# Attention with a gated mixer on one core: two of four probability tiles turned by TensorE instead of by a DMA transpose

## Chip, cores, metric

One core of a Trainium2 chip, with its five engines: TensorE (PE), VectorE (DVE), ScalarE (ACT), GpSimd (POOL) and SyncE (SP), which issues most of the transfers. The metric is the device time of one execution in microseconds (us); lower is better. Each engine has its own instruction queue and works through it in order.

## What is computed

```python
kv_pool = kv.reshape(B, H // r, r, W // r, r, C).mean(axis=(2, 4))   # r = 4
k = v = kv_pool.reshape(B, -1, C) @ w_sr                             # 768 keys
s = scale * (q @ k.transpose(0, 2, 1))
s = s - s.max(-1, keepdims=True)
a = np.exp(s)
a /= a.sum(-1, keepdims=True) + 1e-09
x = a @ v                                                            # attention
gate = sigmoid(sum(conv_w[k] * x_padded[:, k:k + S] for k in range(5)))
out = (gate * (x @ w_val)) @ w_out
```

There are 4 batches of 12288 queries with 128 channels; each batch has 768 keys. Everything is float32. Values and probabilities enter the second product as pairs of float16 numbers, a high and a low half, so that little is lost.

## The kernel before

**Groups, tiles and steps.** A group is 512 queries; there are 96 groups, 24 to a batch, numbered by `gi`. A group has four tiles (`j` = 0 to 3) of 128 queries. The main loop (line 442) has one step for each tile, 384 in all. The order of the work is written out by hand, in that loop, and each engine's queue has it in this order. In the step of tile `j` of group `gi` stand, as far as they concern the change:

- On TensorE: `g_val` (L361, in step 1, a 128x512 float32 product of x and w_val for group gi-4), the score of the *next* tile (`score`, L251: six matmuls into a `[128, 768]` float32 PSUM tile `s`, of which there are three), in step 2 `g_out` (L371, the product with w_out), and a part of the product of probabilities and values for group gi-2 (`av_part`, L303). That product is 18 matmuls of 512 columns, cut into 6, 3, 3 and 6 for steps 0 to 3; the last part stands at the head of step 3, the others at the end of their steps.
- On VectorE: `g_h` in step 2 (L366), the row maximum of this tile (`row_max`, L257), the low half of the *previous* tile's probabilities (`p_lo`, L288), in step 3 `g_x` (L322: scales av by 1/z into x), and in step 1 `norm` of the group before (L270 and L271: z plus 1e-9, reciprocal).
- On ScalarE: exp of this tile, in place in PSUM, which also sums its rows into a column of z (`expo`, L263), then the high half of this tile's probabilities times 2^15, as float16 into an SBUF tile `hl` (`p_hi`, L282). Besides these it has `tap` (L330, steps 0 and 2), tanh (L357, step 1), the evacuation of the output (L381, step 3) and the rounding of q (L239, step 3).
- On GpSimd: the rest of the convolution over x (L332, L341) and the low part of q (L243).
- On SP: q's loads, the stores, and the following transfers.

**The turn of the probabilities.** The scores have queries on partitions, and the product with the values needs keys on partitions. `hl` holds high and low halves of two tiles, `[128, 2, 2, 768]` float16, in three buffers. After the low half of tile 1 and of tile 3, SP issues a DMA transpose of both tiles into `pt` (L294). There are two transposes a group; the last two tiles of the run are turned by one transpose each, 193 in all. `p_lo` is also the last reader of the PSUM tile `s`, so the score three tiles later waits for it.

**1/z on all partitions.** `norm` leaves the reciprocals as `[128 queries, 4 tiles]`; a DMA writes them to DRAM (`rd`, L272, in step 1), and a second one reads them back as one row, broadcast to 128 partitions (`rb`, L277, in step 3). `g_x` reads `rb` a group later.

**PSUM.** Eight banks: three `s` tiles of two banks, one bank for `av`, and one for everything else (`misc`, tile `m`): `g_val`, `g_out` and, when a new batch comes up, the projection of its keys and values. A new user of `misc` waits for the last reader of the one before.

**New batches.** In each batch's second group and after it, small steps prepare the next batch: one in each step 3 (pooling, products), the splits into high and low parts follow in step 0, `low()` after `p_lo` on VectorE.

**After the loop** (line 509 on) the last five groups are finished in another hand-written order.

Of the kernel before, what the change touches and what calls it, by code (L numbers as in the profile page):

```python
# [16 lines left out]
P = 128  # L17
GQ = 512
NT = GQ // P


class Group:
# [2 lines left out]

@with_exitstack
def attn_moe_kernel(ctx, tc, qT, kvT, w_sr, w_moe, outT):
    """qT, outT: [B, C, N]; kvT: [B, R, C, keys * R]; w_moe: [C, C + C + taps], the columns of
    w_val, w_out and conv_w transposed, as float64 bits (int64) or float32."""
    nc = tc.nc  # L30
    B, C, N = qT.shape
    NK, RR = kvT.shape[3] // R, R * R
# [14 lines left out]
    kvp = ctx.enter_context(tc.tile_pool(name="kvp", bufs=4))  # L47
    keys = ctx.enter_context(tc.tile_pool(name="keys", bufs=2))
    io = ctx.enter_context(tc.tile_pool(name="io", bufs=2))
    hlp = ctx.enter_context(tc.tile_pool(name="hlp", bufs=3))  # L50
    ptp = ctx.enter_context(tc.tile_pool(name="ptp", bufs=4))
    work = ctx.enter_context(tc.tile_pool(name="work", bufs=2))
    xp = ctx.enter_context(tc.tile_pool(name="xp", bufs=3))
# [8 lines left out]

    ident = const.tile([P, P], F32, name="ident")
    make_identity(nc, ident)
    wsr = const.tile([C, C], F32, name="wsr")
    wm = const.tile([C, NW], F32, name="wm")
    wval, wout, cwt = wm[:, 0:C], wm[:, C:2 * C], wm[:, 2 * C:]

    def load_moe():
        """Loads the weights; the steps that make float32 of float64's bits, rounded to nearest."""  # L70
        if w_moe.dtype == F32:
            nc.sync.dma_start(out=wm, in_=w_moe)
            return []
        raw = kvp.tile([C, HALF * R], F32, name="rows0", bufs=1).bitcast(I32)[:, :2 * NW]
        rest = kvp.tile([C, HALF * R], F32, name="rows1", bufs=1)
        nc.sync.dma_start(out=raw, in_=w_moe.bitcast(I32))
        words = raw.rearrange("c (n w) -> c w n", w=2)
        lo, hi = words[:, 0], words[:, 1]
        sign, ex, a, t = (rest.bitcast(I32)[:, i * NW:(i + 1) * NW] for i in range(4))
        low = rest[:, 4 * NW:5 * NW]  # L80
        v = nc.vector

        def two(out, in_, s1, op0, s2, op1):
            return lambda: v.tensor_scalar(out=out, in0=in_, scalar1=s1, scalar2=s2,
                                           op0=op0, op1=op1)

        def one(out, in_, s1, op):
            return lambda: v.tensor_single_scalar(out=out, in_=in_, scalar=s1, op=op)

        def both(out, x, y, op):  # L90
            return lambda: v.tensor_tensor(out=out, in0=x, in1=y, op=op)

        return [
            two(ex, hi, 20, ALU.logical_shift_right, 0x7FF, ALU.bitwise_and),
            two(ex, ex, -896.0, ALU.add, 0.0, ALU.max),
            two(ex, ex, 255.0, ALU.min, float(1 << 23), ALU.mult),
            two(a, hi, 0xFFFFF, ALU.bitwise_and, 3, ALU.logical_shift_left),
            two(t, lo, 29, ALU.logical_shift_right, 7, ALU.bitwise_and),
            both(a, a, t, ALU.bitwise_or),
            one(a, a, 0x3F800000, ALU.bitwise_or),  # L100
            one(sign, hi, -2147483648, ALU.bitwise_and),
            both(a, a, sign, ALU.bitwise_or),
            one(t, lo, 0x1FFFFFFF, ALU.bitwise_and),
            two(low, t, 2.0 ** -52, ALU.mult, 0.0, ALU.add),
            both(low.bitcast(I32), low.bitcast(I32), sign, ALU.bitwise_or),
            both(low, low, a.bitcast(F32), ALU.add),
            both(wm, low, ex.bitcast(F32), ALU.mult),
        ]
# [53 lines left out]
        return high, low  # L162

    def column_scale(st):
        """Steps for the power of two that brings the largest value of each column to
        [2^14, 2^15), on a diagonal, and what takes it and P's 2^15 out again."""
        big = small.tile([C, 1], F32, name="big")
        pw = small.tile([C, 1], F32, name="pw")
        up = small.tile([C, 1], I32, name="up")
        st["down"] = keys.tile([C, 1], F32, name="down")  # L170
        st["diag"] = keys.tile([C, C], F32, name="diag", bufs=1)
        v = nc.vector
        return [
            lambda: v.tensor_reduce(out=big, in_=st["vt"], axis=AX.X, op=ALU.max,
                                    apply_absolute_value=True),
            lambda: v.tensor_single_scalar(out=pw.bitcast(I32), in_=big.bitcast(I32),
                                           scalar=0x7F800000, op=ALU.bitwise_and),
            lambda: v.tensor_scalar_max(out=pw, in0=pw, scalar1=2.0 ** -90),
            lambda: v.tensor_scalar(out=up, in0=pw.bitcast(I32), scalar1=-1.0,
                                    scalar2=float(268 << 23), op0=ALU.mult, op1=ALU.add),  # L180
            lambda: v.tensor_scalar_mul(out=st["diag"], in0=ident, scalar1=up.bitcast(F32)),
            lambda: v.tensor_scalar_mul(out=st["down"], in0=pw, scalar1=2.0 ** -29),
        ]
# [35 lines left out]
        return steps + value_steps(st)  # L219

    def load_pair(g, n, parts=1):
        """Loads q for groups g and n with one transfer, or as many as parts."""
        q = io.tile([C, 2, GQ], F32, name="q")
        g.q, n.q = q[:, 0], q[:, 1]

# [29 lines left out]
    def row_max(g, j):  # L255
        nm = small.tile([P, 1], F32, name="nm")
        nc.vector.tensor_reduce(out=nm, in_=g.s[j], axis=AX.X, op=ALU.max, negate=True)  # L257
        g.nm[j] = nm

    def expo(g, j):  # L260
        if j == 0:
            g.z = small.tile([P, NT], F32, name="z")
        nc.scalar.activation(out=g.s[j], in_=g.s[j], func=AF.Exp, bias=g.nm.pop(j),  # L263
                             accum_out=g.z[:, j:j + 1])

    def norm(g):
        ze = small.tile([P, NT], F32, name="ze")
        r = small.tile([P, NT], F32, name="r")
        g.rd = dram.tile([P, NT], F32, name="rd")
        nc.vector.tensor_scalar_add(out=ze, in0=g.z, scalar1=1e-9)  # L270
        nc.vector.reciprocal(out=r, in_=ze)  # L271
        nc.sync.dma_start(out=g.rd, in_=r)  # L272

    def norm_rows(g):
        g.rb = work.tile([C, GQ], F32, name="rb", bufs=3)
        row = g.rd.rearrange("(o p) j -> o (p j)", o=1)
        nc.sync.dma_start(out=g.rb, in_=row.broadcast_to([C, GQ]))  # L277

    def p_hi(g, j):
        if j % 2 == 0:  # L280
            g.hl = hlp.tile([P, 2, 2, NK], F16, name="hl")
        nc.scalar.activation(out=g.hl[:, j % 2, 0], in_=g.s[j], func=AF.Copy, scale=2.0 ** 15)  # L282
        g.h2[j] = g.hl

    def p_lo(g, j, width=2):
        """The low half of tile j; then the transpose of the last `width` tiles."""
        hl = g.h2.pop(j)
        nc.vector.scalar_tensor_tensor(out=hl[:, j % 2, 1], in0=g.s.pop(j), scalar=2.0 ** 15,  # L288
                                       in1=hl[:, j % 2, 0], op0=ALU.mult, op1=ALU.subtract)
        if j == 1:  # L290
            g.pt = ptp.tile([P, NT, 2 * NCH, P], F16, name="pt")
        if j % 2 or width == 1:
            j0, i0 = j + 1 - width, j % 2 + 1 - width
            nc.sync.dma_start_transpose(  # L294
                out=g.pt[:, j0:j + 1].rearrange("p j k q -> p (j k) q"),
                in_=hl[:, i0:i0 + width].rearrange("p j a k -> p (j a k)"))

    AV_ORDER = [(v, k, a) for k in range(NCH) for v, a in (("vh", 0), ("vl", 0), ("vh", 1))]

# [17 lines left out]
        g.tap = {}  # L317

    def g_x(g, av, c0=0, c1=GQ):
        tiles = lambda a: a.rearrange("c (j p) -> c j p", p=P)  # L320
        rows = g.rb.rearrange("c (p j) -> c j p", j=NT)[:, c0 // P:c1 // P]
        nc.vector.scalar_tensor_tensor(out=tiles(g.x[:, HALO + c0:HALO + c1]), in0=tiles(av),  # L322
                                       scalar=g.st["down"], in1=rows,
                                       op0=ALU.mult, op1=ALU.mult)

    def tap(g, k, eng):
# [66 lines left out]
    for b in range(B):  # L393
        for i in range(NG):
            g = Group()
            g.i, g.b, g.t0, g.st = len(groups), b, i * GQ, states[b]
            g.s, g.nm, g.h2 = {}, {}, {}
            groups.append(g)
    G = len(groups)

# [37 lines left out]
    def drip():  # L438
        if trickle:
            trickle.pop(0)()  # L440

    for t in range(NT * G):
# [13 lines left out]
            mg.m = g_val(mg, misc())  # L456
        if nxt:
            score(nxt, (j + 1) % NT)
        if mg and j == 3:
            out_tile(mg)  # L460
            g_evac(mg, mg.m)
# [9 lines left out]
            high = None  # L471
        row_max(cur, j)
        expo(cur, j)
        p_hi(cur, j)
        drip()
        if prev:
            p_lo(prev, (j - 1) % NT, 1 if t == NT * G - 1 else 2)
        if low and (j == 0 or t < NT):
            low()
            low = None  # L480
        drip()
        if avg and j == 3:
            new_x(avg, xg, nc.gpsimd.tensor_copy)
# [3 lines left out]
        if xg and j == 2:  # L487
            tap(xg, 3, nc.scalar)
            g_conv(xg)
        if at(gi - 1) and j == 1:  # L490
            norm(at(gi - 1))
        if at(gi - 1) and j == 3:
            norm_rows(at(gi - 1))
        if at(gi + 2) and j == 3:
            g_qh(at(gi + 2))
# [10 lines left out]
    def bank():  # L506
        return ps_s.tile([P, 1024], F32, name="s")

    p_lo(n1, NT - 1, 1)
    norm(n1)  # L510
    av_part(n2, 0)
    store_pair(n5)
    n4.m = g_val(n4, misc())
# [67 lines left out]
```

## Time and profile before

| what | value |
|---|---|
| time, median of 3 runs | 1233.57 us (1228.01 to 1247.42) |
| span of the profiled execution | 1223.5 us |
| instructions | 15077 |
| DMA moved | 253.19 MB, mean 207 GB/s |
| HBM read and written | 75.83 MB, 25.36 MB |
| mean granted clock of TensorE | 0.954 |

The span goes from the first to the last instruction of one profiled execution; its own time is not listed apart, and the three runs lie 4.5 to 23.9 us above the span, the median 10.1. On a page of the profile, the first part gives each engine's busy time, its share of the span and its number of instructions. The second part cuts the span in 40 equal slices and gives busy tenths. The DMA row there is the mean busy share of the sixteen DMA engines. The third part has the DMA queues: packets, megabytes, and the time their packets took as a share of sixteen engines' span. The fourth follows the chain that ended last backwards. The fifth has groups of equal instructions with busy time and the mean duration of one in ns, then idle time in front of them. In the list of waits each row has who waited for whom, the total in us, how often, and the longest. In a timeline each row is start, duration, engine, line, operation, output from inputs, how many; a bracket gives the idle time in front and who ended it. Consecutive instructions on one engine overlap a little in the records, so the distance of two starts is the time that one takes in a full queue.

### The profile page before, as it was taken

What the parts mean: (1) busy time and instruction counts of PE and PEld (TensorE: products, weight loads), DVE (VectorE), ACT (ScalarE), POOL (GpSimd) and SP (SyncE); (2) the same over time, 40 slices, a digit from 0 to 9 for tenths busy, and PEclk for the clock granted to TensorE, in tenths of its full rate; (3) what the DMA queues carried; (4) which work ended last, traced back from release to release, by engine and by line L of the source; (5) the groups of instructions that cost most, each with busy time, mean ns of one, the idle gap of its engine ahead of it and who ended that gap; (6) DMA issues with size and microseconds to landing.
All of it is one profiled execution on the core that took longest, in us unless ns stands there. A gap on an engine that the chain in (4) does not pass through costs nothing.

```text
span 1223.5 us, 15077 instructions
## 1 busy us (share of the span) xinstructions
PE 1023.3 (84%) x4502; PEld 622.8 (51%) x4502; DVE 1001.5 (82%) x1251; ACT 940.1 (77%) x1657; POOL 814.2 (67%) x872
## 2 busy tenths in 40 slices
PE   1878886789898789789997878886989999999885
PEld 0644454455564445455555545553555555655552
DVE  5977885799987778699998868776998987988884
ACT  1867785688886778688897768766988988988981
POOL 1165775676785676576777657665867877877871
PEclk9899898899999989899999989898999999999998
DMA  8799999999999999999999999999999999999994
GB/s 251 141 216 203 213 218 167 205 211 201 204 227 227 219 210 214 208 204 212 210 222 225 210 195 226 208 188 194 204 223 207 200 220 213 211 220 212 227 195 116
DMA packets 650321, 253.19 MB, mean 207 GB/s; under 512 B 613632, under 2 KB 622208, under 8 KB 650240
## 3 DMA queue, kind: packets, MB, share of 16 engines
q1 hardware_dynamic: 647648, 238.08, 95.3%
q0 software_dynamic: 2592, 14.16, 7.4%
q8 instruction: 36, 0.59, 0.2%
q14 instruction: 45, 0.37, 0.1%
HBM read 75.83 MB, written 25.36 MB: 83 GB/s over the span
## 4 chain that ended last, share of the span: by engine, by line
DMA 49%; PE 27%; DVE 14%; ACT 5%; issue 3%; SPq 1%; DVEq 0%; ACTq 0%
DMA pt<-hl 47%; PE av L303 13%; PE s L251 7%; DVE nm L257 4%; PE m L361 4%; DVE hl L288 4%; DVE x L322 3%; ACT hl L282 3%; PE m L371 2%; ACT s L263 2%; DVE ze L270 1%; DMA kvt<-in_kv 1%; DVE h L366 1%; DMA rb<-rd 1%; SPq L294 1%
## 5 line engine op out<-in xcount | busy, mean ns | idle before, releaser
L341 POOL TENSOR_TENSOR sum<-sum,tap 128x512 f32<-128x512 f32 x282 | 362.0, 1284 | 330.3 <-ACT tap L330 315.7
L303 PE MATMUL av<-pt,vh 128*128 128x512 f16 x1140 | 400.6, 393 | 106.7 <-DMA pt<-hl 101.5
L288 DVE SCALAR_TENSOR_TENSOR hl<-s,hl 128x768 f16<-128x768 f32 x384 | 365.9, 953 | 113.4 <-ACT hl L282 111.9
L263 ACT ACTIVATE s<-s,nm 128x768 f32<-128x768 f32 x384 | 335.1, 873 | 135.8 <-DVE nm L257 134.8
L282 ACT ACTIVATE hl<-s 128x768 f16<-128x768 f32 x384 | 311.5, 811 | 94.8 <-DMA pt<-hl 83.9
L257 DVE TENSOR_REDUCE nm<-s 128x1 f32<-128x768 f32 x384 | 364.6, 950 | 12.8 <-PE s L251 12.6
L251 PE MATMUL s<-kh,qh 128*128 128x512 f32 (+1 forms) x768 | 280.9, 447 | 45.2 <-DVE hl L288 41.5
L303 PEld LDWEIGHTS <-vh 128*128 128x128 f16 x1164 | 115.8, 99 | 279.1 <-issue 143.0
L303 PE MATMUL av<-pt,vl 128*128 128x512 f16 x570 | 223.3, 392 | 0.0
L251 PEld LDWEIGHTS s<-kh,qh 128*128 128x128 f32 x768 | 142.1, 195 | 136.1 <-issue 91.4
L251 PE MATMUL s<-kl,qh 128*128 128x512 f32 (+1 forms) x768 | 200.6, 343 | 0.0
L251 PE MATMUL s<-kh,ql 128*128 128x512 f32 (+1 forms) x768 | 200.3, 342 | 0.0
L332 POOL TENSOR_SCALAR tap<-x,wm 128x512 f32<-128x512 f32 x282 | 195.6, 747 | 0.2
L243 POOL TENSOR_TENSOR ql<-q,qh 128x512 fp32r<-128x512 f32 x96 | 121.8, 1268 | 53.0 <-ACT qh L239 53.0
L322 DVE SCALAR_TENSOR_TENSOR x<-av,down,rb 128x512 f32<-128x512 f32 x95 | 108.2, 1139 | 48.6 <-PE av L303 28.6
L330 ACT ACTIVATE tap<-x,wm 128x512 f32<-128x512 f32 x188 | 133.9, 713 | 0.0
L251 PEld LDWEIGHTS s<-kl,qh 128*128 128x128 f32 x768 | 120.3, 192 | 18.1 <-DVE kl L158 0.5
L251 PEld LDWEIGHTS s<-kh,ql 128*128 128x128 f32 x768 | 120.4, 192 | 17.1
L341 POOL TENSOR_TENSOR sum<-tap,tap 128x512 f32<-128x512 f32 x94 | 125.2, 1332 | 0.0
L371 PE MATMUL m<-h,wm 128*128 128x512 f32 x188 | 100.1, 614 | 20.8 <-DVE h L366 20.8
L361 PE MATMUL m<-x,wm 128*128 128x512 f32 x188 | 107.1, 654 | 0.0
L303 PEld LDWEIGHTS <-vl 128*128 128x128 f16 x582 | 58.1, 100 | 67.9 <-issue 35.7
(58 smaller groups left out, 638.8 us busy)
## 6 DMA issues: line engine op xcount, KB each, us to landing
rb<-rd SPq DMA_DIRECT2D x96, 256.0 KB, 4.8
q<-in_q SPq DMA_DIRECT2D x47, 512.0 KB, 5.6
out<-o SPq DMA_DIRECT2D x46, 512.0 KB, 3.3
rows<-in_kv POOLq DMA_DIRECT2D x18, 768.0 KB, 9.4
kvt<-in_kv SPq DMA_DIRECT2D x16, 384.0 KB, 5.7
rows<-in_kv SPq DMA_DIRECT2D x6, 768.0 KB, 7.2
pt<-hl SPq DMA_TRANSPOSE x193, 7.0
rd<-r SPq DMA_DIRECT2D x96, 2.0 KB, 2.7
```

The costliest lines, as they stand in the source:

```text
L251: nc.tensor.matmul(s[:, c0:c1], a[:, sl], k[:, c0:c1], start=(i == 0), stop=(i == 2))
L257: nc.vector.tensor_reduce(out=nm, in_=g.s[j], axis=AX.X, op=ALU.max, negate=True)
L263: nc.scalar.activation(out=g.s[j], in_=g.s[j], func=AF.Exp, bias=g.nm.pop(j), accum_out=g.z[:, j:j + 1])
L282: nc.scalar.activation(out=g.hl[:, j % 2, 0], in_=g.s[j], func=AF.Copy, scale=2.0 ** 15)
L288: nc.vector.scalar_tensor_tensor(out=hl[:, j % 2, 1], in0=g.s.pop(j), scalar=2.0 ** 15, in1=hl[:, j % 2, 0], op0=ALU.mult, op1=ALU.subtract)
L303: nc.tensor.matmul(out, g.st[v][:, k * P:(k + 1) * P], g.pt[:, j0:j1, a * NCH + k], start=(i == 0), stop=(i == len(AV_ORDER) - 1))
L322: nc.vector.scalar_tensor_tensor(out=tiles(g.x[:, HALO + c0:HALO + c1]), in0=tiles(av), scalar=g.st["down"], in1=rows, op0=ALU.mult, op1=A ...
L330: nc.scalar.activation(out=g.tap[k], in_=src, func=AF.Copy, scale=w)
L332: eng.tensor_scalar(out=g.tap[k], in0=src, scalar1=w, scalar2=1.0, op0=ALU.mult, op1=ALU.mult)
L341: nc.gpsimd.tensor_tensor(out=s, in0=acc, in1=g.tap[k], op=ALU.add)
L361: nc.tensor.matmul(m, wval, g.x[:, HALO + c0:HALO + c1], start=True, stop=True)
L371: nc.tensor.matmul(m, wout, h, start=True, stop=True)
```

## The change

With `NX = 2`, tiles 0 and 1 of a group keep the DMA transpose, now one for each group, after the low half of tile 1. Tiles 2 and 3 go another way:

- exp writes its result to a new SBUF tile `pf` (float32, three buffers) instead of back to `s`;
- one step later, after the score of the next tile, TensorE transposes `pf` in six 128x128 pieces into the tile's own PSUM tile `s` (`turn`);
- then `p_hi` and `p_lo` of that tile read the turned tile and write straight into `pt`. `p_hi` of these tiles thus also comes one step later, after the next tile's exp.

The sums z go into one of three constant `[128, 128]` tiles that are cleared at the start. `norm` moves from step 1 to step 0: ScalarE adds 1e-9 in place, TensorE transposes the whole tile into a `misc` bank, VectorE takes the reciprocal of four rows from there, and `rd` is now `[4, 128]`. `norm_rows` moves from step 3 to step 2. `rb` is in the order of the queries, so `g_x` reads it without strides. `hl` has two buffers instead of three. At the end the last tile is turned by TensorE as well.

```diff
+NX = 2
...
-    hlp = ctx.enter_context(tc.tile_pool(name="hlp", bufs=3))
+    hlp = ctx.enter_context(tc.tile_pool(name="hlp", bufs=2))
+    pfp = ctx.enter_context(tc.tile_pool(name="pfp", bufs=3))
...
+    zs = [const.tile([P, P], F32, name=f"z{i}") for i in range(3)]
+    for z in zs:
+        nc.vector.memset(z, 0.0)
...
+    def on_pe(j):
+        return j >= NX
+
     def expo(g, j):
         if j == 0:
-            g.z = small.tile([P, NT], F32, name="z")
-        nc.scalar.activation(out=g.s[j], in_=g.s[j], func=AF.Exp, bias=g.nm.pop(j),
-                             accum_out=g.z[:, j:j + 1])
+            g.z = zs[g.i % len(zs)]
+        if on_pe(j):
+            g.pf[j] = pfp.tile([P, NK], F32, name="pf")
+        nc.scalar.activation(out=g.pf[j] if on_pe(j) else g.s[j], in_=g.s[j], func=AF.Exp,
+                             bias=g.nm.pop(j), accum_out=g.z[:, j:j + 1])
 
     def norm(g):
-        ze = small.tile([P, NT], F32, name="ze")
-        r = small.tile([P, NT], F32, name="r")
-        g.rd = dram.tile([P, NT], F32, name="rd")
-        nc.vector.tensor_scalar_add(out=ze, in0=g.z, scalar1=1e-9)
-        nc.vector.reciprocal(out=r, in_=ze)
+        m = misc()
+        nc.scalar.activation(out=g.z[:, :NT], in_=g.z[:, :NT], func=AF.Copy, bias=1e-9)
+        nc.tensor.transpose(m[:, :P], g.z, ident)
+        r = small.tile([NT, P], F32, name="r")
+        g.rd = dram.tile([NT, P], F32, name="rd")
+        nc.vector.reciprocal(out=r, in_=m[:NT, :P])
         nc.sync.dma_start(out=g.rd, in_=r)
...
+    def turn(g, j):
+        pf = g.pf.pop(j)
+        for k in range(NCH):
+            nc.tensor.transpose(g.s[j][:, k * P:(k + 1) * P], pf[:, k * P:(k + 1) * P], ident)
...
     def p_hi(g, j):
+        if on_pe(j):
+            out = pt_tile(g)[:, j, :NCH].rearrange("p k q -> p (k q)")
+        else:
+            if j == 0:
+                g.hl = hlp.tile([P, NX, 2, NK], F16, name="hl")
+            out = g.hl[:, j, 0]
+        nc.scalar.activation(out=out, in_=g.s[j], func=AF.Copy, scale=2.0 ** 15)
+        g.hi[j] = out
...
+    def p_lo(g, j):
+        if on_pe(j):
+            out = pt_tile(g)[:, j, NCH:].rearrange("p k q -> p (k q)")
+        else:
+            out = g.hl[:, j, 1]
+        nc.vector.scalar_tensor_tensor(out=out, in0=g.s.pop(j), scalar=2.0 ** 15,
+                                       in1=g.hi.pop(j), op0=ALU.mult, op1=ALU.subtract)
+        if j == NX - 1:
             nc.sync.dma_start_transpose(
-                out=g.pt[:, j0:j + 1].rearrange("p j k q -> p (j k) q"),
-                in_=hl[:, i0:i0 + width].rearrange("p j a k -> p (j a k)"))
+                out=pt_tile(g)[:, :NX].rearrange("p j k q -> p (j k) q"),
+                in_=g.hl.rearrange("p j a k -> p (j a k)"))
...
         if nxt:
             score(nxt, (j + 1) % NT)
+        pj = (j - 1) % NT
+        if prev and on_pe(pj):
+            turn(prev, pj)
...
         row_max(cur, j)
         expo(cur, j)
-        p_hi(cur, j)
+        if prev and on_pe(pj):
+            p_hi(prev, pj)
+        if not on_pe(j):
+            p_hi(cur, j)
         drip()
         if prev:
-            p_lo(prev, (j - 1) % NT, 1 if t == NT * G - 1 else 2)
+            p_lo(prev, pj)
         if low and (j == 0 or t < NT):
             low()
             low = None
+        if at(gi - 1) and j == 0:
+            norm(at(gi - 1))
...
-        if at(gi - 1) and j == 1:
-            norm(at(gi - 1))
-        if at(gi - 1) and j == 3:
+        if at(gi - 1) and j == 2:
             norm_rows(at(gi - 1))
...
-    p_lo(n1, NT - 1, 1)
+    turn(n1, NT - 1)
+    p_hi(n1, NT - 1)
     norm(n1)
+    p_lo(n1, NT - 1)
```

More of the change, by code (lines that the diff above doesn't have):

```diff
@@ L275, in norm_rows, with pt_tile @@
         g.rb = work.tile([C, GQ], F32, name="rb", bufs=3)
-        row = g.rd.rearrange("(o p) j -> o (p j)", o=1)
+        row = g.rd.rearrange("(o j) p -> o (j p)", o=1)
         nc.sync.dma_start(out=g.rb, in_=row.broadcast_to([C, GQ]))
-    def p_hi(g, j):
[L280 to L293, printed above, removed]
+    def turn(g, j):
+        pf = g.pf.pop(j)
+        for k in range(NCH):
+            nc.tensor.transpose(g.s[j][:, k * P:(k + 1) * P], pf[:, k * P:(k + 1) * P], ident)
+    def pt_tile(g):
+        if g.pt is None:
+            g.pt = ptp.tile([P, NT, 2 * NCH, P], F16, name="pt")
+        return g.pt
+    def p_hi(g, j):
+        if on_pe(j):
[14 more added lines that the diff above has]
+        if j == NX - 1:
             nc.sync.dma_start_transpose(
-                out=g.pt[:, j0:j + 1].rearrange("p j k q -> p (j k) q"),
-                in_=hl[:, i0:i0 + width].rearrange("p j a k -> p (j a k)"))
+                out=pt_tile(g)[:, :NX].rearrange("p j k q -> p (j k) q"),
+                in_=g.hl.rearrange("p j a k -> p (j a k)"))
     AV_ORDER = [(v, k, a) for k in range(NCH) for v, a in (("vh", 0), ("vl", 0), ("vh", 1))]
@@ L319, in g_x @@
     def g_x(g, av, c0=0, c1=GQ):
[L320 to L323, printed above, removed]
+        nc.vector.scalar_tensor_tensor(out=g.x[:, HALO + c0:HALO + c1], in0=av,
+                                       scalar=g.st["down"], in1=g.rb[:, c0:c1],
                                        op0=ALU.mult, op1=ALU.mult)
@@ L396, in attn_moe_kernel @@
             g.i, g.b, g.t0, g.st = len(groups), b, i * GQ, states[b]
-            g.s, g.nm, g.h2 = {}, {}, {}
+            g.s, g.nm, g.pf, g.hi, g.pt = {}, {}, {}, {}, None
             groups.append(g)
```

## The prediction

> **What bounds the kernel now.** First the page, top to bottom.
>
> ```profile
> PE 1023.3 (84%) x4502; PEld 622.8 (51%) x4502; DVE 1001.5 (82%) x1251; ACT 940.1 (77%) x1657; POOL 814.2 (67%) x872
> ...
> DMA  8799999999999999999999999999999999999994
> ...
> q1 hardware_dynamic: 647648, 238.08, 95.3%
> q0 software_dynamic: 2592, 14.16, 7.4%
> ...
> DMA 49%; PE 27%; DVE 14%; ACT 5%; issue 3%; SPq 1%; DVEq 0%; ACTq 0%
> ...
> rb<-rd SPq DMA_DIRECT2D x96, 256.0 KB, 4.8
> ...
> pt<-hl SPq DMA_TRANSPOSE x193, 7.0
> ```
>
> No engine is above 84%, while the two DMA queues together account for 103% of the sixteen DMA engines' span, and half of the chain that ended last is DMA. The 193 transposes are named as the cause by the list of waits:
>
> ```profile
> PE av L303 <- DMA pt<-hl: 101.5, 61, 5.5
> ACT hl L282 <- DMA pt<-hl: 83.9, 47, 9.9
> ...
> DVE pool L118 <- DMA kvt<-in_kv: 8.7, 10, 4.3
> ```
>
> Then the pace. `g_x` runs once a group on VectorE, so its starts are a clock of groups (the source view of L322 and VectorE's timeline):
>
> ```profile
> 57.31 1.11 DVE L322 SCALAR_TENSOR_TENSOR x<-av,down,rb 128x512 f32<-128x512 f32 x1
> ...
> 621.32 1.14 DVE L322 SCALAR_TENSOR_TENSOR x<-av,down,rb 128x512 f32<-128x512 f32 x1 [0.33 <-PE av L303]
> ...
> 631.26 1.14 DVE L322 SCALAR_TENSOR_TENSOR x<-av,down,rb 128x512 f32<-128x512 f32 x1
> ...
> 1188.39 1.13 DVE L322 SCALAR_TENSOR_TENSOR x<-av,down,rb 128x512 f32<-128x512 f32 x1
> ```
>
> From group 2 (57.31) to group 95 (1188.39) are 93 periods: 12.16 us each. Where no transposition is late (621.32 to 631.26) a period is 9.94 us. So some 2.2 us of each group are DMA; halving the transposes frees them. The question is what the new order of work costs.
>
> **The new order, followed through one group.** Call a group's tiles 0 to 3; a prime marks the next group. The queues run in program order. Before, everything that tile t needs from ScalarE (exp, high half) is done in its own step, so in step t+1 VectorE goes from the row maximum straight to the low half of tile t. After, the high half of tiles 2 and 3 moves one step later: behind the turn on TensorE, and on ScalarE *behind the exp of the next tile*, which needs the row maximum of that next tile. And `norm` moves to step 0: ScalarE adds 1e-9 after three activations, TensorE turns z, VectorE takes the reciprocal. TensorE stands at the turn of z until ScalarE is there, and the next `g_val` waits for the reciprocal as well (one `misc` buffer). This closes a loop through a whole group, so I add up its two legs.
>
> *TensorE's leg*, from the reciprocal on. The chain of waits shows the same instructions back to back:
>
> ```profile
> 614.78 0.86 PE m L361 x2
> 615.64 1.05 PE s L251 x6
> 616.69 0.66 PE av L303 x3
> 617.36 1.06 PE s L251 x6
> 618.42 0.86 PE m L371 x2
> 619.28 1.96 PE av L303 x9
> ```
>
> These are `g_val`, score of tile 2', av part 1, score of 3', `g_out`, av parts 2 and 3: 614.78 to 621.24, 6.45 us. Then come the score of tile 0'' (1.05) and the turn of tile 2'. No turn is in the trace of before; nearest is the matmul of the same shape and type (L188):
>
> ```profile
> L188 PE MATMUL m<-diag,vt x48: 272/275/421, 39.2 to 948.7; 128*128 128x128 f32 x48
> ...
> 632.04 0.83 PE L188 MATMUL m<-diag,vt 128*128 128x128 f32 x6
> 632.63 0.60 PE L251 MATMUL s<-kh,qh 128*128 128x512 f32 x2
> ```
>
> Six go in 0.59 us (632.04 to 632.63), 0.10 each, and the last record outlasts its slot by 0.17. A turn of a tile is six such instructions if one transpose is one instruction: 0.60 + 0.17. Below: the av matmul streams 512 columns in 0.22 us (1.96 for nine), so 128 columns can't be expected under 0.054, six in 0.32. Above: six records one after another, 6 x 0.275 = 1.65 (two instructions each would be 1.2, in between). I take 0.60, the nearest shape. Leg: 6.45 + 1.05 + 0.77 = 8.27 us.
>
> The Trainium skill ("TensorE: Matmul & The Clock Gate", Part 4: PE-mode transpose) gives about 390 ns for a 128x128 bf16 transpose alone and about 275 ns in one kernel. By 275 a turn would be 1.65 us, by 390 ns 2.3; the trace agrees with 275 as the length of a record, but not as the spacing, which is 0.10.
>
> *ScalarE's and VectorE's leg*, from the turn of tile 2' to the reciprocal, by starts in the timelines:
>
> ```profile
> 622.38 0.95 DVE L257 TENSOR_REDUCE nm<-s 128x1 f32<-128x768 f32 x1
> 623.25 0.94 DVE L288 SCALAR_TENSOR_TENSOR hl<-s,hl 128x768 f16<-128x768 f32 x1
> 624.11 0.95 DVE L257 TENSOR_REDUCE nm<-s 128x1 f32<-128x768 f32 x1
> ...
> 626.85 0.18 DVE L271 RECIPROCAL r<-ze 128x4 f32<-128x4 f32 x1
> 626.94 0.67 DVE L366 SCALAR_TENSOR_TENSOR h<-th,m 128x512 f32<-128x512 f32 x1
> 627.53 0.95 DVE L257 TENSOR_REDUCE nm<-s 128x1 f32<-128x768 f32 x1
> ```
>
> ```profile
> 623.36 0.88 ACT L263 ACTIVATE s<-s,nm 128x768 f32<-128x768 f32 x1
> ...
> 624.39 0.81 ACT L282 ACTIVATE hl<-s 128x768 f16<-128x768 f32 x1
> 625.10 0.71 ACT L330 ACTIVATE tap<-x,wm 128x512 f32<-128x512 f32 x1
> ```
>
> High half of 2' 0.81 to its end, and 0.03 to VectorE's start: 0.84. Low half to the next start 0.87 (623.25 to 624.11). `g_x` 1.06 (621.32 to 622.38). Row maximum of 0'' to its end and over to ScalarE 0.98. Exp of 0'' 1.03 (623.36 to 624.39). High half of 3' 0.71, of 0'' 0.71 (624.39 to 625.10). Then the three operations that before doesn't show: z plus 1e-9 on ScalarE, the turn of z, the reciprocal of 4x128 out of PSUM:
>
> ```profile
> L316 ACT COPY x<-x 128x4 f32<-128x4 f32 x2 | 0.4, 177 | 0.0
> ```
>
> The same 128x4 on ScalarE takes 0.18 here; with half an L188 slot more for the start I take 0.22. The turn of z is one LDWEIGHTS slot and one record, 0.10 + 0.275 = 0.37. The reciprocal of 4 elements is 0.18 (626.85); 128 elements at the rate of `g_x` (512 in 1.06) add up to 0.26, I take 0.24. Together 0.83, between 0.6 and 1.2. Sum of the leg: 0.84 + 0.87 + 1.06 + 0.98 + 1.03 + 1.42 + 0.83 = 7.03 us.
>
> **The loop: 8.27 + 7.03 = 15.3 us a group against 12.16.** Inside it, other work is covered. The turn of tile 3' (score of 1'' 1.05 and 0.77 after the low half of 2', whose end is 1.8 into the leg) is done at 3.6; its high half could start at 4.8. Av part 0 (six at 0.22) ends at 4.8, before z at 6.4. The row maxima, low halves and `g_h` of steps 1 and 2 are VectorE's in TensorE's leg: 4 x 0.87 + 0.59 = 4.1 of 8.27. If that cover went, this is the rival of VectorE below.
>
> **What is removed** gains nothing beside this: 96 `ze` instructions and, each group, one transposition, which none waits for once the group lasts 15.3. Moved DMAs: `rd` leaves in step 0, the remaining transposition in step 2, with `rb` behind it on SP; `rb` needs 4.8 us and is read a group later. One transposition a group lands in 7.0 us, so two `hl` buffers suffice. Three clearings of z at the start fall in VectorE's wait for the first keys (up to 4.3 us by the list of waits): nothing. Exp of tiles 2 and 3 into SBUF: by the row of L282 (0.81 against 0.88) up to 0.07 less, off the loop.
>
> **Batch changes.** In eight groups for each of three new batches, 24 in all, VectorE has one more instruction in step 0 ahead of the reciprocal:
>
> ```profile
> L133 DVE TENSOR_REDUCE pool<-rows 128x192 f32<-128x768 f32 x12 | 11.3, 942 | 0.0
> ...
> L200 DVE TENSOR_TENSOR vl<-m,vh 128x384 f16<-128x384 f32 x8 | 4.4, 551 | 0.0
> ```
>
> A pooling (12 in all) comes after the low half of 3', at 1.71 from the start of that tile's high half, and ends at 2.6, where z was ready at 2.0: 0.6. A low half of keys or values (12) holds the `misc` buffer until 2.3 and z's turn behind it: 0.65. Together 24 x 0.63 = 15 us.
>
> **Start and end.** The first three groups have five steps with the new bubble (exp and high half between row maximum and low half, 1.03 + 0.84) and had slack; I add 6 us to 58.3 (57.31 and a slot of `g_x`, the end of group 2). Group 3 has no `g_val` and `g_out`: 15.3 - 1.72 = 13.6. At the end the last two single transposes go away:
>
> ```profile
> 1195.64 0.38 PE L303 MATMUL av<-pt,vh 128*128 128x512 f16 x1
> ...
> 1200.01 1.11 DVE L322 SCALAR_TENSOR_TENSOR x<-av,down,rb 128x512 f32<-128x512 f32 x1 [8.12 <-DMA rb<-rd]
> ```
>
> This `g_x` waited for `rb`, stuck on SP behind transposes; its av was done at 1196.0, so 4 us less: 34 (from 1188.39 and its slot, 1189.4, to 1223.5) becomes 30. **Sum of the span:** 58.3 + 6 + 13.6 + 92 x 15.3 + 30 + 15 = 1530 us against 1223.5. The profiled execution is known here by its span; the median of the runs, 1233.57, is 10 above it. Forecast: 1540 us.
>
> **Rivals.** *Turns that don't overlap.* The six transposes run record after record (1.65, upper bound): the loop is 16.35, the time 1540 + 92 x 1.05 = 1637. For it: no transpose has run here. Against: L188's spacing. The 275 ns of the Trainium skill (the part cited above) would come to the same time.
>
> *TensorE's leg is covered*, and only VectorE's loop is left: steps 3 and 0 with their bubble, 0.98 + 1.03 + 0.84 + 0.87 + 1.06 = 4.78 and 0.98 + 1.03 + 1.42 + 0.83 = 4.26, step 1 1.74, step 2 0.59 + 1.74: 13.1. Time 58.3 + 6 + 93 x 13.1 + 30 + 15 + 10 = 1338. It needs 2.2 us less on TensorE between z and the turn of 2'. Against: the seven rows above stand back to back.
>
> *A slower clock.* In the 7.03 us leg TensorE works about 3 us.
>
> ```profile
> 73.73 0.61 PE L303 MATMUL av<-pt,vh 128*128 128x512 f16 x1 [5.02 <-DMA pt<-hl]
> 74.13 0.63 PE L303 MATMUL av<-pt,vl 128*128 128x512 f16 x1
> ```
>
> After an idle 5.02 us the av spacing was 0.40 to 0.43, twice the usual, for some 3 us. Each such stretch costs 1.6 us; once a group: 1540 + 92 x 1.6 = 1687. Against: the new gaps are under 2 us.
>
> *Faster.* TensorE alone sets the pace: `g_val`, `g_out`, four scores, 18 av, two turns, z come to 0.86 x 2 + 1.06 x 4 + 3.9 + 1.2 + 0.4 = 11.5 us, if the waits at ScalarE and VectorE are absorbed. 93 x 0.66 less and 4 at the end: 1168. It decides only if both the high halves are ready when VectorE asks and z's turn does not hold TensorE, that is, if these queues don't run in written order. Against: the ScalarE and VectorE rows above are in the order of the code.
>
> **How the numbers follow.** The loop of both legs 0.64 (1470 to 1600); turns without overlap 0.12; TensorE covered 0.10; slow clock 0.06; TensorE's pace 0.08, of which 0.02 end within 2% because part of the waits stays. 2% is about what a measurement of this kernel tells from no change. Range 1330 to 1640: it takes in VectorE's loop and turns from 0.32 (15.0 us, 1514) to 1.65. Faster 0.06, same 0.02, slower 0.92.
>
> **What would show it.** Right: `g_x` every 15.3 us or so; ScalarE waiting some 2 us for the turn before the high half of tile 2; TensorE waiting over 1 us a group for z; VectorE's busy share near 60%; the DMA row no longer at nine throughout; six transposes spaced 0.10. Wrong: transposes on TensorE still few in the waits and a period under 12 us; or a period near 13.1, with VectorE waiting only for exp and high half; or av spacing of 0.43 each group.

## The result

The changed kernel takes 1688.17 us (median of 4 runs, 1685.49 to 1692.2), the kernel before 1230.79 us beside it. The ratio is 1.3734, with a 95% interval of 1.3674 to 1.3794: 37% slower. The ratios here and below compare the fast executions of each kernel; the kernel before has some that take 1.5% longer and more. The forecast of a slowdown held; the time lies 148 us above the 1540 forecast and above the range's end of 1640.

The page of the profile after: busy times, the queue that carries the transposes (q1) and the chain that ended last.

```profile
PE 1288.5 (76%) x5750; PEld 815.2 (48%) x5750; DVE 955.0 (57%) x1158; ACT 949.9 (56%) x1753; POOL 813.6 (48%) x872
...
q1 hardware_dynamic: 336576, 162.56, 40.9%
...
PE 57%; DVE 17%; ACT 16%; issue 9%; DMA 1%; SPq 0%; DVEq 0%; ACTq 0%
```

DMA is out of the chain: 49% of it before, 1% now. No engine took its place as a full one; VectorE and ScalarE are busy 57 and 56%. The chain runs through TensorE, VectorE and ScalarE in turn, which is what a loop of waits looks like. The list of waits of the same kernel names its links (who waits and for what, us in all, waits, the longest):

```profile
DVE pt L319 <- ACT pt L310: 576.9, 191, 4.4
...
ACT pt L310 <- PE s L296: 202.6, 96, 2.2
...
PE s L256 <- DVE pt L319: 170.6, 95, 1.9
PEld m L387 <- DVE r L284: 116.6, 89, 1.8
PEld m L281 <- ACT z L280: 106.5, 84, 2.7
```

VectorE stands before the low half of a turned tile twice a group, 3 us each (576.9 in 191 waits). ScalarE waits 2.1 us a group for the turn of tile 2 (96 waits), TensorE for z and for the reciprocal (about 100 us each).

Here is the loop itself, in the chain of waits of the changed kernel, from one reciprocal to the next and on (start, us, what):

```profile
499.34 0.96 DVE r L284
...
500.34 1.98 PE m L387 x2
502.32 1.82 PE s L256 x6
504.14 0.66 PE av L331 x3
504.80 1.05 PE s L256 x6
505.86 0.86 PE m L397 x2
506.71 1.94 PE av L331 x9
508.65 1.06 PE s L256 x6
509.72 0.67 PE s L296 x6
510.41 0.82 ACT pt L310
...
512.13 0.74 DVE x L348
512.87 0.88 DVE nm L262
513.77 0.54 ACT s L274
...
516.31 0.34 PE m L281
516.67 0.96 DVE r L284
...
517.67 1.12 PE m L387 x2
518.80 1.05 PE s L256 x6
```

These are the two legs of the prediction, instruction for instruction: `g_val` (L387), score (L256), av (L331), score, `g_out` (L397), av, score, turn (L296), high half (L310), low half (in the gap), `g_x` (L348), row maximum (L262), exp (L274), two high halves, z (L281), reciprocal (L284). From 499.34 to 516.67 are 17.33 us, where 15.3 were summed.

### The profile page after: what moved, and what is told of

Read it like the earlier page. It is cut to its first block, busy times and chain, and to the rows that moved or that the text cites. A ratio compares the mean times of both kernels' runs of the same rounds, so it can differ in the third digit from the quotient of the medians.

```text
span 1686.3 us, 17134 instructions
## 1 busy us (share of the span) xinstructions
PE 1288.5 (76%) x5750; PEld 815.2 (48%) x5750; DVE 955.0 (57%) x1158; ACT 949.9 (56%) x1753; POOL 813.6 (48%) x872
## 4 chain that ended last, share of the span: by engine, by line
PE 57%; DVE 17%; ACT 16%; issue 9%; DMA 1%; SPq 0%; DVEq 0%; ACTq 0%
PE s L256 22%; PE av L331 16%; ACT pt L310 9%; PE m L387 8%; DVE r L284 5%; DVE nm L262 5%; PE m L397 5%; DVE x L348 4%; PE s L296 4%; ACT s L274 4%; ACT hl L310 3%; PE m L281 2%; DMA kvt<-in_kv 1%; DVE pt L319 1%; DVE pool L123 0%
## 5 line engine op out<-in xcount | busy, mean ns | idle before, releaser
L319 DVE SCALAR_TENSOR_TENSOR pt<-s,pt 128x768 f16<-128x768 f32 x192 | 183.8, 957 | 576.9 <-ACT pt L310 576.9
L256 PE MATMUL s<-kh,qh 128*128 128x512 f32 (+1 forms) x768 | 328.5, 513 | 175.9 <-DVE pt L319 170.6
L262 DVE TENSOR_REDUCE nm<-s 128x1 f32<-128x768 f32 x384 | 359.2, 935 | 89.9 <-PE s L256 89.3
L331 PE MATMUL av<-pt,vh 128*128 128x512 f16 x1140 | 404.3, 396 | 0.5 <-DVE x L348 0.5
L274 ACT ACTIVATE s<-s,nm 128x768 f32<-128x768 f32 x192 | 168.1, 875 | 314.1 <-DVE nm L262 314.1
L256 PEld LDWEIGHTS s<-kh,qh 128*128 128x128 f32 x768 | 158.9, 218 | 303.5 <-DVE pt L319 195.0
L310 ACT ACTIVATE pt<-s 128x768 f16<-128x768 f32 x192 | 154.4, 805 | 202.7 <-PE s L296 202.6
L274 ACT ACTIVATE pf<-s,nm 128x768 f32<-128x768 f32 x192 | 172.5, 898 | 147.9 <-DVE nm L262 147.9
L331 PE MATMUL av<-pt,vl 128*128 128x512 f16 x570 | 224.8, 394 | 0.0
L256 PE MATMUL s<-kl,qh 128*128 128x512 f32 (+1 forms) x768 | 222.2, 374 | 0.0
L387 PE MATMUL m<-x,wm 128*128 128x512 f32 x188 | 141.1, 841 | 102.1 <-DVE r L284 99.0
L256 PE MATMUL s<-kh,ql 128*128 128x512 f32 (+1 forms) x768 | 217.6, 367 | 0.0
L331 PEld LDWEIGHTS <-vh 128*128 128x128 f16 x1164 | 118.3, 102 | 153.6 <-issue 57.5
L319 DVE SCALAR_TENSOR_TENSOR hl<-s,hl 128x768 f16<-128x768 f32 x192 | 180.2, 938 | 0.3 <-ACT hl L310 0.3
L296 PE MATMUL s<-ident,pf 128*128 128x128 f32 x1152 | 158.0, 273 | 0.0
L310 ACT ACTIVATE hl<-s 128x768 f16<-128x768 f32 x192 | 155.4, 810 | 3.1
L256 PEld LDWEIGHTS s<-kl,qh 128*128 128x128 f32 x768 | 136.6, 217 | 21.4 <-DVE kl L163 0.5
L256 PEld LDWEIGHTS s<-kh,ql 128*128 128x128 f32 x768 | 134.7, 214 | 20.7
L296 PEld LDWEIGHTS s<-ident,pf 128*128 128x128 f32 x1152 | 134.6, 140 | 9.0
```

Of the source, the lines that this page charges most:

```text
L256: nc.tensor.matmul(s[:, c0:c1], a[:, sl], k[:, c0:c1], start=(i == 0), stop=(i == 2))
L274: nc.scalar.activation(out=g.pf[j] if on_pe(j) else g.s[j], in_=g.s[j], func=AF.Exp, bias=g.nm.pop(j), accum_out=g.z[:, j:j + 1])
L296: nc.tensor.transpose(g.s[j][:, k * P:(k + 1) * P], pf[:, k * P:(k + 1) * P], ident)
L310: nc.scalar.activation(out=out, in_=g.s[j], func=AF.Copy, scale=2.0 ** 15)
L319: nc.vector.scalar_tensor_tensor(out=out, in0=g.s.pop(j), scalar=2.0 ** 15, in1=g.hi.pop(j), op0=ALU.mult, op1=ALU.subtract)
L331: nc.tensor.matmul(out, g.st[v][:, k * P:(k + 1) * P], g.pt[:, j0:j1, a * NCH + k], start=(i == 0), stop=(i == len(AV_ORDER) - 1))
```

## The experiments

Every kernel below starts from the changed kernel, unless it says otherwise. "1/z the old way" means the old `norm`, `norm_rows` and `g_x`: sum and reciprocal on VectorE in step 1, rows read with strides. Experiments 1 to 5, 7 and the second kernel of 9 rest on one execution each; the four of the changed kernel lie within 0.4%.

**1. TensorE kept busy in its waits.** Eight matmuls after the turn of tile 2, four before the turn of z, into a free `misc` bank.

```diff
+    def filler(st, m, n):
+        for _ in range(n):
+            nc.tensor.matmul(m, st["vh"][:, :P], st["vl"][:, :GQ], start=True, stop=True)
...
         m = misc()
+        if 2 <= g.i < G - 2:
+            filler(groups[g.i - 1].st, m, 4)
...
             g_evac(mg, mg.m)
+            filler(mg.st, misc(), 8)
```

> Twelve matmuls a group whose results nobody reads fill two waits of TensorE (eight after the turn of tile 2, four before the turn of z); they lie inside the waits if one takes 0.22 us. Theory (the clock: after the idle stretch g_val takes 2.0 us in place of 0.86 and the next score 1.8 in place of 1.05, because the granted clock is down to about 0.63 there): both fall back, the period goes from 17.3 to about 15.4 us and the time from 1688 to about 1510 (1490 to 1545), with a granted clock near 1. Rival (TensorE restarts slowly after any wait for VectorE, whatever its load): g_val stays at 2.0 us and the time within 1% of 1688, or rises if the extra matmuls stick out.

Measured: 1590.68 us, granted clock 0.992 against 0.922. In the chain of waits of this kernel the pair behind the reciprocal is at its full speed:

```profile
525.23 1.13 PE m L393 x2
526.36 1.05 PE s L256 x6
```

So the lower clock was the reason for 1.98 and 1.82, and 97 us go with it; 1104 additional matmuls made the kernel faster. (1.13 is still more than the 0.86 of the same pair in a full queue.) The gain is half of the 178 us expected, because the slow stretch wasn't in every group: the changed kernel has periods of 17.33 and of 15.72 us (`g_x` at 494.80, 512.13 and 527.85 in its VectorE timeline). In the trace's record of the granted clock, a stretch at half clock falls in 71 of the 92 periods of its loop (from the second `g_x` on), and in 2 of the 92 of this kernel. Here 67 periods have 15.7 us (`g_x` at 503.97 and 519.69); 24 of the other 25 belong to batch changes. Those with a low half of keys or values take 17.4 us at full clock, where the changed kernel takes 16.4; there the fillers cost some 11 us in twelve periods.

**2. The reciprocal before the turn.**

```diff
+        nc.vector.reciprocal(out=g.z[:, :NT], in_=g.z[:, :NT])
         nc.tensor.transpose(m[:, :P], g.z, ident)
...
-        nc.vector.reciprocal(out=r, in_=m[:NT, :P])
+        nc.vector.tensor_copy(out=r, in_=m[:NT, :P])
```

> The reciprocal is taken of z as 128x4 before TensorE turns it, and VectorE only copies the 4x128 out of PSUM. Theory (the reciprocal's time goes by the elements of a partition, 0.95 us for 128 against 0.18 for 4, and it stands in the loop): 0.95 us leave the loop and about 0.45 come in (0.18 and a handover of 0.05, a copy near 0.2); period 17.3 to 16.8, time 1688 to about 1640. Rival (the reciprocal is slow because it reads PSUM or only 4 partitions): the copy takes as long, 0.9 us, and the time rises to about 1710.

Measured: 1589.23 us, clock 0.937. The groups of this kernel by line and shape, then those of the changed kernel:

```profile
L285 DVE COPY r<-m 4x128 f32<-4x128 f32 x96 | 26.8, 279 | 42.4 <-PE m L282 42.4
L281 DVE RECIPROCAL z<-z 128x4 f32<-128x4 f32 x96 | 16.1, 167 | 0.0
```

```profile
L284 DVE RECIPROCAL r<-m 4x128 f32<-4x128 f32 x96 | 90.7, 944 | 23.7 <-PE m L281 23.7
```

The theory's term is right: 4x128 out of PSUM is copied in 0.28 us and takes 0.94 as a reciprocal, so it is the operation on 128 elements a partition that costs, and not reading PSUM or only four partitions. The time fell by 99 us, twice the 48 expected. The clock went up as well, from 0.922 to 0.937, so the shorter wait also counted there. The periods set the two apart: without a half-clock stretch and outside of batch changes they are 15.3 us against 15.7, 0.4 x 92 = 37 us. The other 62 us come from fewer such stretches (52 of 92 periods against 71), which are also cheaper (0.7 us against 1.55 in a plain group).

**3. Both edits.**

> Both edits together. Theory (two terms of one loop were sized wrong, nothing else): the gains add, period near 14.9 us, below the 15.3 that the prediction summed, because g_x without strides takes 0.74 us and not 1.06; time about 1465 (1440 to 1500). Rival (a second loop of about the same length stands behind the first): the sum of the two single gains is not reached, the time stays above 1520.

Measured: 1549.29 us, clock 0.998, period 15.33 us in its VectorE timeline (`g_x` at 506.19 and 521.52).

At full clock the reciprocal's edit is worth 0.4 us a group, 41 us in all, about what was expected of it. The period of 14.9 and the time of 1465 were missed: my expectation took 1.9 us off every group for the clock, but a slow stretch costs 1.6 and did not come in every group. The sum of the single gains (196) was not reached (139), since each of them takes part of the same slow stretches away. The rival's number (above 1520) is met, but its cause is not what the chain shows: it is still the same loop, only with VectorE's low half of tile 3 between the high half and the reciprocal, and no second loop.

**4. The turns alone**, 1/z the old way.

> The turns of tiles 2 and 3 alone: 1/z goes the old way (sum and reciprocal on VectorE in step 1, rows read with strides). Theory (the turn of z closes the loop through TensorE; without it VectorE's own order, row maximum, exp, high half, low half, sets the pace in steps 3 and 0): period about 13.6 us, time about 1370 (1320 to 1420). Rival (the turns themselves hold TensorE, z does not matter): time above 1500.

Measured: 1468.49 us, between the two. Periods are 14.1 and, with a half-clock stretch, 14.9 us. The chain of waits shows how the loop closes without z:

```profile
496.65 0.97 DVE pt L317
...
497.67 1.32 PE s L256 x6
...
522.12 2.18 PE s L256 x6
524.30 1.28 PE s L294 x6
```

The score of tile 2' waits for the low half of tile 3, which holds one of the three PSUM tiles. This wait takes the place of z's. The last two lines are a score and a turn at half clock, 2.18 and 1.28 us: the clock drops here too (0.951 on the mean). Both theories fall short: the turn of z is not the only thing that closes a loop. Without it another one stands at 14.1 us, through TensorE as well; with it the loop has 15.72, both at full clock.

**5. 1/z alone**: all tiles by DMA in pairs (`on_pe` returns False, `p_hi` and `p_lo` as before, three `hl` buffers), z turned by TensorE in step 0.

> The other part alone: all four tiles are turned by DMA in pairs as before, and only 1/z is turned by TensorE in step 0, with rb read without strides. Theory (z's turn is harmful by closing a loop with the late high halves; with the high halves in their own steps the loop is about 6.45 and 1.05 on TensorE, then 0.98, 1.03, 0.71, 0.22, 0.37 and 0.95, some 11.8 us, below the DMA pace of 12.16): time near before, 1225 to 1290. Rival (z's turn alone brings most of the loss): above 1400.

Measured: 1370.46 us against 1229.0 for the kernel before, run beside it: between the theory (to 1290) and the rival (above 1400). The theory's sum was wrong, and the chain shows what it left out; the last row is from the list of waits:

```profile
480.57 21.88 DMA pt<-hl
...
502.50 2.74 PE av L327 x6
505.23 0.23 PE m L281
...
505.48 0.96 DVE r L284
...
DVE r L284 <- PE m L281: 193.1, 95, 21.8
```

DMA is still the bound (q1 at 88.0% of the longer span), so av part 0 waits for a late transpose. z's turn stands behind it on TensorE, the reciprocal behind that on VectorE, and row maxima and low halves behind the reciprocal; without low halves no transpose can be issued. VectorE stands 193 us before the reciprocal, up to 21.8 at once, where the kernel before has no such wait. The new link turns a late transpose into a stop of VectorE too. How much of the 141 us is this link is not shown: the granted clock was also the lowest of all runs, 0.910, and the six av matmuls above took 2.74 us at a clock of 0.50, where they take 1.31 in experiment 8.

**6. Another order.** The turns alone, 1/z the old way, the turn ahead of the score on TensorE, the high half ahead of the next exp on ScalarE.

```diff
+        pj = (j - 1) % NT
+        if prev and on_pe(pj):
+            turn(prev, pj)
         if mg and j == 1:
             mg.m = g_val(mg, misc())
         if nxt:
             score(nxt, (j + 1) % NT)
-        pj = (j - 1) % NT
-        if prev and on_pe(pj):
-            turn(prev, pj)
...
         row_max(cur, j)
-        expo(cur, j)
         if prev and on_pe(pj):
             p_hi(prev, pj)
+        expo(cur, j)
```

> Turns of tiles 2 and 3 on TensorE, 1/z the old way, and a new order: the turn stands before the next score on TensorE, and the high half of the turned tile before the next exp on ScalarE. Theory (the loss is the order, not the price of the turns): VectorE no longer waits for exp and high half, TensorE's own work sets the pace, 1.72 and 4.2 and 3.9 and 1.2, about 11.0 to 11.5 us a group, under the 12.16 of before because half of the transposes are gone; time 1110 to 1180. Rival (the turns on TensorE cost more than the DMA transposes whatever the order): above 1233.

Measured: 1238.47 us, ratio to before 1.0114 (1.0019 to 1.0209). The same turns in another order cost 230 us less than in experiment 4. Some 35 us of this are clock, by its periods with and without a half-clock stretch (38 of 92 have one there; here the clock is 0.995). The gain below 1180 did not come. The time lies above 1233, where the rival had it, although its reason does not hold: the order did count, by most of the 230 us.

**7. Which half of the order?** Only ScalarE's order (second block), only TensorE's (first block).

> The turns alone, 1/z the old way, with only ScalarE's order changed: the high half of the turned tile stands before the next exp, while TensorE keeps the turn behind the score. Theory (the exp of 1.03 us and the row maximum of 0.98 between low half and high half are the loss in step 0; in step 3 TensorE is late anyway, since score and turn follow the av part): between the two kernels, time about 1340 (1290 to 1400). Rival (only the place of the turn on TensorE counts): within 2% of 1468.

> The fourth of the four orders: the turns alone, 1/z the old way, the turn ahead of the score on TensorE, ScalarE as in the change (next exp first, then the high half). Theory (with TensorE never late, VectorE's own loop is left, row maximum, exp, high half, low half in steps 3 and 0, summed at 13.6 us): time about 1350 (1300 to 1400). Rival (ScalarE's order decides and TensorE's place of the turn gives nothing without it): within 2% of 1468.

Measured: 1444.45 us with ScalarE's order alone, 1343.15 with TensorE's alone. So of the four orders, none 1468, ScalarE's 1444, TensorE's 1343, both 1238. The first expectation missed, and its rival was met (within 2% of 1468): with the turn behind the score, ScalarE's queue stands before the high half and the next exp stands behind it, as the list of waits of that kernel shows (142.5 us in experiment 4):

```profile
ACT pt L308 <- PE s L294: 378.7, 192, 3.8
```

ScalarE's order counts mostly together with TensorE's: 24 us without it, 105 with it. The second expectation met its number, but not its reason. VectorE's own loop, expected at 13.6 us, is not what is left; the chain has 13.02 us from one `g_x` to the next and goes through TensorE:

```profile
518.10 1.11 DVE x L348
...
521.84 0.97 DVE pt L317
...
522.85 1.31 PE s L256 x6
...
528.71 0.67 PE s L294 x6
...
529.40 0.82 ACT pt L308
...
531.12 1.12 DVE x L348
```

It is the loop of experiment 4, the score of tile 2' behind the low half of tile 3, without the 1.06 us of the score that stood ahead of the turn there: 14.1 less 1.06 is 13.0. That the prediction's rival "TensorE's leg is covered" also has 13.1 is chance; it is summed without TensorE and with z's turn.

**8. Without the addition of 1e-9**, in the kernel of experiment 6 and, as a control, in the kernel before.

```diff
-        nc.vector.tensor_scalar_add(out=ze, in0=g.z[:, :NT], scalar1=1e-9)
-        nc.vector.reciprocal(out=r, in_=ze)
+        nc.vector.reciprocal(out=r, in_=g.z[:, :NT])
```

> The kernel of the new order (turn before the score, high half before the exp, 1/z the old way) without the addition of 1e-9: z is at least 1, where float32 has no room for it. In that kernel's chain the addition stands with 1.04 us a group between the low half of tile 0 and g_h, on which g_out and the av parts wait. Theory (it is a term of that loop): period from about 12.6 to 11.6, time from 1238 to about 1150 (1130 to 1190). Rival (TensorE, busy 91%, has no more to give): above 1200.

> The kernel before without the addition of 1e-9, as a control: theory (DMA sets its pace of 12.16 us) within 1% of before, 1220 to 1240; rival (the addition's waits, 88.7 us in all, stand in the pace) 1150 to 1200.

Measured: 1222.74 us (16 less than experiment 6, not 90, and in the rival's range above 1200; ratio to before 1.0082, 1.0057 to 1.0106), and 1210.82 for the control (0.9935 of before, 0.9885 to 0.9986: within 1%, as the theory said, though the time lies 9 us below the 1220 it named). The chain of the first shows that the next loop stood right behind, on TensorE and ScalarE:

```profile
520.22 0.67 PE s L292 x6
...
520.91 0.81 ACT pt L306
521.72 0.89 ACT pf L274 x2
...
522.66 0.88 PE s L292 x6
```

Turn of tile 2, its high half, then exp of tile 3, then the turn of tile 3: TensorE stands for 1.77 us in each group, since two turned tiles follow one another. Its work, 10.3 us, and this wait make the period of 12.1.

**9. One turned tile**, `NX = 3`: in the new order of experiment 8, and in the order of the change.

> The same with one tile of four (tile 3) turned by TensorE, and the other three by one DMA transpose. Theory (TensorE is the next bound; a group's turn is 0.67 us and one wait for ScalarE less): period about 10.9, time about 1080 (1040 to 1130). Rival (DMA: a pair costs about 4.2 us of the engines, by the shares 40.9 and 4.8 percent of 17.6 us a group after and 103 percent of 12.2 before, so three tiles make some 10.1 us with the rest, and the transposes come late again): 1150 or more.

> The changed kernel with one number changed, NX = 3: tiles 0 to 2 go by one DMA transpose, tile 3 is turned by TensorE, order and z as in the change. Theory (the loop through z stays, without turn, high half, low half of tile 2 in it: 6.45 and 1.05 on TensorE, row maximum 0.98, exp 1.03, two high halves 1.42, z 0.22, 0.37 and 0.95 give 12.6 us at full clock, up to 1.6 more where the clock is down): time between 1290 and 1430. Rival (two turned tiles in a row were the loss, z's place does not matter): near the 1127 of one tile in the new order.

Measured: 1127.41 us, ratio to before 0.9295 (0.9272 to 0.9317), and 1313.31 us. The first beats both kernels by 7% or more; in a stretch of six groups TensorE is busy nearly all the time at full clock, with DMA below its limit (columns: PE, PEld, DVE, ACT, POOL busy, clock, DMA share, GB/s):

```profile
492.00:557.00 65.00, 64.57 (x315) 40.59 (x313) 57.71 (x77) 59.02 (x107) 50.51 (x55) 1.00 0.87 176
```

The six periods there are 10.97 us on average (`g_x` from 491.61 to 557.45) and those of the whole loop 11.12, against 10.9 summed. The time is 47 above the 1080 expected, at the upper end of its range: in some groups `g_x` waits for `rb` (73.9 us in all) and ScalarE for q (30.9), and DMA is back in the chain with 14%. The second has a period of 12.68 us (`g_x` at 512.09 and 524.77) against 12.6 summed.

The same split of tiles takes 186 us more with the order and the 1/z of the change: these two together count, not only the number of turned tiles.

## Why the prediction was right, and where it was wrong

**Right: the mechanism.** "This closes a loop through a whole group" is what the chain shows, link by link, and the removal of the DMA bound paid nothing, as said. The same loop without one turn was summed at 12.6 and came out at 12.68 (experiment 9). What the prediction did not see is the second loop right behind it, the score of tile 2' that waits for the low half of tile 3, 14.1 us at full clock (experiment 4).

**Right: the price of a turn.** A turn was put at 0.77 us, six transposes at the spacing of L188 and the end of the last record; it takes 0.69 until the high half starts (509.72 to 510.41), with records as long as L188's:

```profile
L296 PE MATMUL s<-ident,pf 128*128 128x128 f32 x1152 | 158.0, 273 | 0.0
```

The rival of turns without overlap, 1.65 us, is out. The 275 ns that the Trainium skill gives ("TensorE: Matmul & The Clock Gate", Part 4: PE-mode transpose) for bf16 in one kernel agrees with this float32 record of 273. In a full queue one takes 0.11 us (0.67 for six).

**Wrong: the clock.** The step that failed is a term put at nothing: the rival "A slower clock" had 0.06 and was left out of the sum because "the new gaps are under 2 us". They are: the longest wait of TensorE for a low half is 1.9 us in the list above (the weight load's for z is 2.7 at most). The clock fell all the same. In the trace's record the granted clock changes only on a grid of 3.41 us. The windows view of the changed kernel, cut on this grid, has TensorE's busy time behind the comma and the clock in the third column from the right:

```profile
497.06:500.48 3.42, 1.61 (x8) 0.58 (x7) 2.10 (x3) 2.99 (x7) 2.74 (x4) 1.00 0.10 41
500.48:503.89 3.41, 3.41 (x8) 2.02 (x8) 2.17 (x3) 1.80 (x3) 0.46 (x1) 0.50 0.39 154
...
514.13:517.55 3.42, 1.74 (x9) 0.58 (x6) 1.83 (x3) 3.25 (x7) 3.34 (x5) 1.00 0.90 149
517.55:520.96 3.41, 3.29 (x15) 2.21 (x16) 3.40 (x6) 1.88 (x4) 0.99 (x1) 1.00 0.41 84
```

TensorE's records fill 3.6 of some 7 us in the sparse leg, cut by waits of 1.9, 0.8 and 1.0 us. Two legs alike differ in how they fall on the grid: the first leaves a stretch with 0.47 of its time filled (1.61 of 3.42), and the next one is at half clock; the second is divided into 0.55 (1.86 of 3.41 from 510.72) and 0.51, and the clock stays. Over the whole trace, none of the 327 stretches at full clock that TensorE fills by half or more is followed by half clock; of 63 filled by 0.445 to 0.5, 57 are, and all 17 below that. The trace of before held a warning that was not read, here cut on its own grid, with 0.46 filled and the clock down in the next stretch:

```profile
42.46:45.87 3.41, 1.56 (x8) 0.91 (x6) 3.06 (x7) 2.95 (x5) 0.00 (x0) 1.00 1.12 210
45.87:49.28 3.41, 2.87 (x10) 2.61 (x11) 3.41 (x7) 2.91 (x7) 0.00 (x0) 0.50 0.86 117
```

The border is not sharp: of 10 such stretches between 0.445 and 0.5 in that kernel, only 2 were followed by half clock.

The Trainium skill ("TensorE: Matmul & The Clock Gate", Part 1, "What's actually happening") has the clock at half rate after an idle window of about 3.4 us. The trace agrees with the half (0.50 in the view above), but no wait inside this loop was as long as that. Nearer to the trace is the same page's section "A second HAM failure mode: psum-queue depth-cycling", where frequent short idles between groups of matmuls let the clock swing; the prediction did not weigh it, and it gives no number from which the loss could have been worked out. Experiment 1 settles the cause: with the waits filled, 2 of 92 periods have a half-clock stretch, and 97 us are gone.

The rival's own time, 1687, is 1 us from the measured one by chance. It had a slow stretch in every group, 147 us, where 71 of 92 had one, and the other terms below make up the rest.

**Wrong: the reciprocal.** Its term was 0.24 us, bounded above by 0.26 at the rate of `g_x`; it took 0.95. The rate of a multiplication was no bound for it. With it the three operations on z take 1.51 us (516.16 to 517.67) where 0.83 was summed and 1.2 the upper bound. `g_val` was taken from a full queue, 0.86; behind a wait it takes 1.12 at full clock. The other way, `g_x` was summed at 1.06 and takes 0.74 now that `rb` is read without strides: that part of the change was overlooked as a gain. Together the loop at full clock is 15.72 and not 15.3.

**The bill**, forecast to result, 148 us: lower clock 111 (the 71 periods with a half-clock stretch, each against those without one, some 1.5 to 1.6 us; the 97 of experiment 1 are less, mainly by the 11 that its fillers cost); loop at full clock 0.42 x 92 = 39; start 9 (the first `g_x` begins at 72.0 against 63.2, which is 58.3 + 6 less its own slot). Against these, the end is 3 shorter, and the time lies 2 us above the span of its own execution and not 10, 8 less. The batch changes were right: at full clock a pooling group takes 0.53 us more and one with a low half of keys or values 0.72, where 0.6 and 0.65 were summed. VectorE's share was put near 60% and is 57%.

## What to carry to other kernels

When a bound is removed, follow the written order of each queue through one full period and add up the loop: a step moved behind another engine's next item can cost more than the transfer it replaced. The same turns took 1468 us in one order and 1238 in another, and one turned tile instead of two, in that order and without the addition of 1e-9, gave 1127. In a loop with gaps, judge TensorE's clock by its load and not by the longest gap: in these traces half clock followed on stretches of 3.41 us of which TensorE's records filled less than about half.

## What the hardware showed beside that

- A reciprocal's time went by the elements of a partition: 0.17 us for 128x4 in SBUF, 0.94 for 4x128 out of PSUM, some 6 ns for each further element if the two places cost the same; a copy of the same 4x128 took 0.28.
- The granted clock moved in steps of 3.41 us between 1.00 and 0.50; no stretch of the changed kernel with 0.5 or more of TensorE's records was followed by 0.50, and 74 of 80 with less were.
- `g_x` over 128x512 took 1.14 us with strided operands and 0.74 without.
- More TensorE work made a kernel faster: 1104 matmuls whose results nobody reads, 97 us less.
